# Block 0's first transform reads the raw rows: twelve products per column group and a wider table, in place of additions on VectorE and four products

## The chip, the cores and the metric

The kernel runs on one core of one Trainium2 chip. The metric is the device time of one execution in microseconds. The core has five engines that run side by side, each with a queue of its own that it works off in order: TensorE (PE; its weight loads are listed apart as PEld), VectorE (DVE), ScalarE (ACT), GpSimd (POOL) and SyncE (SP). In this kernel SyncE's queue issues almost all transfers between HBM and the on-chip memory; ScalarE's queue issues three at the start. Products land in PSUM, and VectorE or ScalarE must copy them out before their buffer is used again.

## The reference

The output mixes two branches over the same x (2048 rows of 512 numbers, bf16). One is a filter in the frequency domain, the other a layer norm followed by a two-layer network over the rows. A gate per row weighs them.

```python
x = A_x                                              # [1, 2048, 512]
g = sigmoid((x * gate_w).sum(-1, keepdims=True))
X = rfft2(x.astype(float32), axes=(-2, -1)) * (A_w_r + 1j * A_w_i)
a = irfft2(X, s=(2048, 512), axes=(-2, -1)).astype(bfloat16)
h = layernorm(x)
u = gelu(einsum("bsd,sf->bdf", h, w1) + b1)          # F = 1792
b = (einsum("bdf,fs->bds", u, w2) + b2).transpose(0, 2, 1)
out = g * a + (1 - g) * b
```

## The kernel before

The 2048 rows are split as `row = 512 q + 4 p + r`: p is the partition (0 to 127), and q and r run over 0 to 3. "Block r" is the 512 rows with the same r: four row tiles of 128 x 512, one for each q. Row tile j is 4 q + r. The kernel loads x block by block (`t["x"]`, L365 and L367), with the table of that block (`t["ta"]`, L368) and a part of w1 (`t["wa"]`, L378).

For each block four things are done:

- **Statistics and h.** VectorE takes mean and variance of each row tile (L462, L463). ScalarE takes the root (L472), VectorE the reciprocal and the shift (L476, L477). The normalised row tile h is written by VectorE for three row tiles (0, 8 and 4; L480) and by ScalarE for the other thirteen (L486).
- **Additions over q.** VectorE combines the four row tiles of a block by a radix-4 butterfly: two operations of 1024 elements (`q4a`, L494 and L495) and two of 512 (`q4b`, L500 and L501). The results stand in four parts of `t["xf", r]`, which lies in the not yet used end of the buffer `gl`.
- **First transform, over the rows (`fa`, L509 to L516).** For each column group dq (128 of the 512 columns) TensorE makes four products: the parts 2 and 3 with 256 table columns each, added in PSUM (L513, L514), and the parts 0 and 1 with 128 each (L515, L516). A PSUM buffer of the kind "fa" (there are two) holds the result of a group, and ScalarE copies it to `t["X"]` (L519).
- **Additions over column groups.** VectorE combines the copies (`d4a` and `d4b`, L526 to L533).

With all four blocks through, VectorE applies a radix-4 step to X for each of two halves lt (1, then 0; L552 to L565). The copy L603 then puts twelve small sums (L584 to L595) into the half lt = 0. Each of sixteen column transforms (`fb`, L621 to L624) puts four products into a buffer "fa" or "fb" (two each), which ScalarE copies to `t["B"]` (L628). Each half has eight of them; the half lt = 1 runs first.

The filter's weights come by many small transfers of SP (`ld_W`, two sets of eighteen). TensorE turns a part of them by a product with a flipped unit matrix (L706, into "fa" and "fb"), and ScalarE copies that out (L710). VectorE then prepares them (`wprep`: L726, L729, L730), multiplies B with them, and goes back over the columns; TensorE's inverse transforms are L838 to L845 over the rows and L912 to L916 over the columns.

The network's first layer is the products of L656 (`m1`), 224 of them with 512 columns, called **hidden products** here. Its sums lie in the PSUM buffers "acc" (four) and "fb" (two: the sums 4 and 5); ScalarE's Gelu empties them (L670). The first 72 hidden products run over twelve row tiles, two at a time, for the first six sums; the next 24 finish these six sums with block 3's row tiles. The second layer is L930 (`m2`), 238 products. The gate is made by VectorE (L679) and ScalarE's sums (L684).

Before the first transform TensorE runs warm-up products on zeros (`warm`, L353).

The order on every queue is fixed when the kernel is built. `add(engine, cost, emit, reads, writes, prio, ...)` records a task with an assumed cost; `Plan.order` plays the tasks through, and takes on each engine, of the tasks that are ready by the assumed costs, the one with the lowest `prio`. On the chip each engine then works through its own list in that order and waits where the data are not there. A change of one cost or `prio` can so move instructions anywhere behind it.

Of the kernel before, what the change touches and what calls it, by code (L numbers as in the profile page):

```python
# [28 lines left out]
    return np.ascontiguousarray(a.astype(ml_dtypes.bfloat16))  # L29


def ti_at(r):
    return (0, 1024, 512, 1920)[r], (512, 896)[r % 2]


def make_tables():

    p = np.arange(P)
    r4 = np.arange(4)
    alt = np.where(p % 2 == 0, 1.0, -1.0)  # L40

    def ang(rows, k, n):
        return 2 * np.pi * ((rows[..., None] * k) % n) / n

    ta = np.zeros((P, 4, 640))
    ti = np.zeros((P, 2946))
    for r in range(4):
        s = 4 * p + r
        for n, k0 in enumerate((0, 2)):
            th = ang(s, k0 + 4 * np.arange(64), S)  # L50
            ta[:, r, n * 128:n * 128 + 64] = np.cos(th)
            ta[:, r, n * 128 + 64:n * 128 + 128] = -np.sin(th)
        ta[:, r, 64] = alt
        th = ang(s, 1 + 4 * (p ^ 96), S)
        ta[:, r, 256:384] = np.cos(th)
        ta[:, r, 384:512] = -np.sin(th)
        ta[:, r, 512:640] = -np.cos(th)

        k = np.where(p < 64, 4 * p, 2 + 4 * (p - 64))
        o, w = ti_at(r)  # L60
        v = ti[:, o:o + w]
        if r % 2:
            sg = np.where(p < 64, 1.0, -1.0)[:, None]
            th = ang(k, s, S)
            v = v.reshape(P, 7, P)
            v[:, 0] = np.cos(th)
            v[:, 1] = sg * np.cos(th)
            v[:, 2] = -np.sin(th)
            v[:, 3] = -sg * np.sin(th)
            v[0, 2:4] = alt * (0.5 ** 0.5 if r == 1 else -(0.5 ** 0.5))  # L70
            th = ang(1 + 4 * (p ^ 96), s, S)
            v[:, 4] = -np.sin(th)
            v[:, 5] = np.cos(th)
            v[:, 6] = np.sin(th)
            ti[:, o:o + w] = v.reshape(P, w)
        else:
            s5 = np.append(s, 512)
            for lt, kk in enumerate((k, 1 + 4 * (p ^ 96))):
                th = ang(kk, s5, S)
                c, n = np.cos(th), -np.sin(th)  # L80
# [24 lines left out]
    tc[:, :, 2] = tc[:, :, 0]  # L105
    cf = np.zeros((P, 4, 2))
    m = np.arange(8).reshape(4, 2)
    for r in range(4):
        cf[m[0, 0], r, 0] = 1.0
        cf[8, r, 0] = (1.0, -1.0)[r % 2]  # L110
        cf[m[1, r % 2], r, 0] = (1.0, -1.0, -1.0, 1.0)[r]
        if r != 2:
            cf[m[2, 0], r, 1], cf[m[3, 0], r, 1] = 1.0, (1.0, -1.0)[r % 2]
        if r != 0:
            cf[m[2, 1], r, 1], cf[m[3, 1], r, 1] = (0.0, -1.0, 1.0, 1.0)[r], (0.0, -1.0, -1.0, 1.0)[r]
    tb = np.concatenate([tb[:, :, 0:2].reshape(P, 384), tc.reshape(P, 768), cf.reshape(P, 8)], 1)

    tg = np.zeros((P, 642))
    sc = 2.0 / (D * S)
    d = np.arange(129)  # L120
    for h in range(2):
        th = ang(2 * p + h, d, D)
        c, n = sc * np.cos(th), -sc * np.sin(th)
        if h == 0:
            c[0], n[0] = sc / 2, 0.0
            tg[:, 0:129], tg[:, 129:256] = c, n[:, 1:128]
        else:
            tg[:, 256:384], tg[:, 384], tg[:, 385:512] = c[:, 0:128], -n[:, 128], n[:, 1:128]
    tg[0, 512:641] = np.where(d % 2 == 0, 1.0, -1.0) * sc / 2
    return {"flip": bf(np.eye(P)[::-1]), "ta": bf(ta), "ti": bf(ti), "tb": bf(tb), "tg": bf(tg)}  # L130


# [103 lines left out]
def tt(n):  # L236
    return 0.07 + n / 1920.0
# [24 lines left out]
def kernel(  # L262
# [42 lines left out]
    def alloc_first():  # L305
        t["eps"] = sb([P, 1], F32, "eps")
        V.memset(t["eps"][:], 1e-5)
        t["x"] = sb([P, 4, 4, D], BF16, "x")
        t["h"] = sb([P, 4, 4, D], BF16, "h")
        t["X"] = sb([P, 2, 4, 2, 4, P], BF16, "X")  # L310
        t["B"] = sb([P, 2, 4, 4, L], BF16, "B")
        t["xp"] = sb([P, 8192], BF16, "xp")
        t["warm"] = t["xp"][:, 0:D]
        V.memset(t["warm"], 0.0)  # L314
        t["s9"] = sb([P, D], BF16, "s9")
        t["b1b"] = sb([P, P], BF16, "b1b")
        t["b2b"] = sb([P, D], BF16, "b2b")
        for k in ("s9", "b1b", "b2b"):
            V.memset(t[k][:], 0.0)
        t["st"] = sb([P, 4096], BF16, "st")  # L320
        t["gl"] = sb([P, NFT, D], BF16, "gl")
        t["W"] = sb([P, 2, 2, 4, 2, WL], BF16, "W")
        t["wn"] = sb([1, 2, WL], BF16, "wn")
        t["ta"] = sb([P, 4, 640], BF16, "rot")
        t["wt"] = sb([P, 2, 4, WL], BF16, "wt")
        t["wpm"] = sb([P, 2, 2, 4, 2], F32, "wpm")
        t["sp"] = sb([P, 4, 2, 4], F32, "sp")
        t["sd"] = sb([P, 2, 2, 2, 4], F32, "sd")
        t["fx"] = sb([P, 4, 2, 4], F32, "fx")
        t["c0"] = sb([P, 2, 4, 2, 2], F32, "c0")  # L330
        t["cm"] = sb([P, 4, 4, 2], F32, "cm")
        t["ce"] = sb([P, 2, 4, 2, 2], F32, "ce")
        for name, shape in (("stats", [P, NJ, nc.vector.BN_STATS_DIM]), ("mv", [P, NJ, nc.vector.BN_AGGR_DIM]),
                            ("rstd", [P, NJ]), ("nmr", [P, NJ]), ("glog", [P, NJ]), ("g", [P, NJ]), ("omg", [P, NJ]),
                            ("ombb2", [P, NJ]), ("b1f", [P, NFT]), ("b2f", [P, NJ])):
            t[name] = sb(shape, F32, name)
# [13 lines left out]
    def warm():  # L350
        pw = ps([P, D], F32, "fa", 2)
        for _ in range(NWARM):
            T.matmul(pw[:], lhsT=t["warm"][:, 0:P], rhs=t["warm"], start=True, stop=True)  # L353
    NWARM = 13
    add("PE", 0.42 * NWARM, warm, reads=["warm", "xs"], writes=["warmed"], prio=-5, alloc=["fa"], free=["fa"])

    def presq():
# [4 lines left out]
    for r in range(4):  # L362
        if r == 0:
            for q in range(4):
                ld([("x", 0, q)], lambda q=q: t["x"][:, q, 0, :], x4[:, q, 0, :], 131072, -9 + 0.1 * q, "SP" if q < 2 else "ACT")  # L365
        else:
            ld([("x", r, q) for q in range(4)], lambda r=r: t["x"][:, :, r, :], x4[:, :, r, :], 524288, 2 * r)  # L367
        ld([("ta", r)], lambda r=r: t["ta"][:, r, :], tabs["ta"][:, r, :], 163840, 2 * r + 0.2)  # L368

    NF = 6  # L370

# [7 lines left out]
        return emit  # L379

    for b in range(2):
        add(("SP", "ACT")[b], 0.5, ld_w1(0, slice(b, 4, 2), (None, A)[b]), writes=[("w1", 0, 4 * b), ("w1", 0, 4 * b + 8)], prio=(0.5, -4)[b],
            alloc=() if b else ["wa"], nbytes=393216, after=[a0])
    for r in range(1, 4):
        add("SP", 0.5, ld_w1(r), writes=[("w1", 0, 4 * q + r) for q in range(4)], prio=2 * r + 0.5, nbytes=786432)
# [61 lines left out]
    for r in range(4):  # L447
# [49 lines left out]
        def q4b(r=r):  # L497
# [1 line left out]
            s = t["st"][:, 0:1024].rearrange("p (m d) -> p m d", m=2)  # L499
            V.tensor_add(xf[:, 0], s[:, 0], s[:, 1])  # L500
            V.tensor_sub(xf[:, 1], s[:, 0], s[:, 1])  # L501
        if r == 0:
            add("DVE", 2 * tt(1024) + 2 * tt(512), lambda: (q4a(0), q4b(0)), reads=xk, writes=[("xf", 0), "st"], prio=-0.5, alloc=["xf"])
        else:
            add("DVE", 2 * tt(1024), q4a, reads=xk, writes=[("xf", r % 2), "st"], prio=1.2 * r + 0.6, alloc=["xf"])
            add("DVE", 2 * tt(512), q4b, reads=["st"], writes=[("xf", r % 2)], prio=1.2 * r + 0.6)

        for dq in range(4):
            def fa(r=r, dq=dq):  # L509
                pa = t["pa", r, dq] = ps([P, 2, 2, P], F32, "fa", 2)  # L510
                ta = t["ta"][:, r, :]
                w = lambda k: t["xf", r][:, k, dq * P:(dq + 1) * P]
                T.matmul(pa[:, 1], lhsT=w(2), rhs=ta[:, 256:512], start=True, stop=False)  # L513
                T.matmul(pa[:, 1], lhsT=w(3), rhs=ta[:, 384:640], start=False, stop=True)  # L514
                T.matmul(pa[:, 0, :, 0:64], lhsT=w(0), rhs=ta[:, 0:128], start=True, stop=True)  # L515
                T.matmul(pa[:, 0, :, 64:128], lhsT=w(1), rhs=ta[:, 128:256], start=True, stop=True)  # L516
            add("PE", mm(128, 128, 256, 256), fa, reads=[("xf", r % 2), ("ta", r)], writes=[("pa", r, dq)], prio=0, alloc=["fa"],
                free=["xf"] if dq == 3 else ())
            add("ACT", act(512), lambda r=r, dq=dq: A.copy(t["X"][:, :, r, :, dq, :], t["pa", r, dq][:]),  # L519
                reads=[("pa", r, dq)], writes=[("X", r, dq)], prio=0, free=["fa"])  # L520

# [491 lines left out]
```

## Time and profile before

| | us |
|---|---|
| median of 3 runs | 135.9 |
| lowest, highest | 135.12, 136.0 |
| the profiled execution, whole | 135.35 |
| span of the profiled execution (first to last instruction) | 133.3 |

The profile is of one execution. Times in it count from the first instruction. A row of the timeline has its start, its duration, the engine, the line of the kernel, the operation, output and inputs by name, how many instructions stand in the row, and in brackets how long the engine sat idle before it and what ended that. Operations of one kind overlap by their ends, so the pace of an engine is the distance between starts.

```profile
## 2 busy tenths in 40 slices
PE   6759999999999999999999999999999999999990
PEld 2244454545444666644445445557766756555590
DVE  2989999999999996399999999997797899999531
ACT  4047699999999999961111035326992966565200
POOL 0000000000000000000000000000000000000000
PEclk9999999999999999999999999999999999999999
DMA  4999999926499456999955900000000003304111
GB/s 133 277 363 392 391 391 380 272 61 135 79 308 360 90 126 174 317 362 416 424 223 193 417 25 2 0 2 5 0 0 0 5 0 157 130 27 162 50 69 38
```

Each digit is the busy share of a slice of 3.3 us in tenths. TensorE has its low slices at the start alone. VectorE is busy nearly throughout, ScalarE in the first half.

### The profile page before, as it was taken

The numbers are of one execution on the slowest core, as the hardware profiler recorded it, in microseconds if no ns is written. First come the engines' busy times: TensorE is split into PE (matmuls) and PEld (weight loads), VectorE is DVE, ScalarE is ACT, GpSimd is POOL, SyncE is SP. The second block draws the span as 40 slices with busy tenths as digits, with TensorE's granted clock in tenths as the row PEclk, the third lists the DMA queues.
The fourth block names the chain that finished last, engine by engine and source line by source line (L and its number), as shares of the span: only waits on it lengthen the run. The fifth ranks groups of instructions, "written<-read, shape, count | busy, mean of one in ns | idle before, by whom it ended". The sixth has DMA issues, their size and how long they took to land.

```text
span 133.3 us, 2162 instructions
## 1 busy us (share of the span) xinstructions
PE 125.3 (94%) x755; PEld 70.6 (53%) x769; DVE 115.0 (86%) x294; ACT 80.4 (60%) x155; POOL 0.2 (0%) x4
## 2 busy tenths in 40 slices
PE   6759999999999999999999999999999999999990
PEld 2244454545444666644445445557766756555590
DVE  2989999999999996399999999997797899999531
ACT  4047699999999999961111035326992966565200
POOL 0000000000000000000000000000000000000000
PEclk9999999999999999999999999999999999999999
DMA  4999999926499456999955900000000003304111
GB/s 133 277 363 392 391 391 380 272 61 135 79 308 360 90 126 174 317 362 416 424 223 193 417 25 2 0 2 5 0 0 0 5 0 157 130 27 162 50 69 38
DMA packets 17206, 23.18 MB, mean 174 GB/s; under 512 B 1174, under 2 KB 14636, under 8 KB 17196
## 3 DMA queue, kind: packets, MB, share of 16 engines
q1 hardware_dynamic: 16636, 22.39, 49.4%
q10 hardware_dynamic: 560, 0.66, 1.4%
q8 instruction: 6, 0.10, 0.3%
q14 instruction: 4, 0.03, 0.1%
HBM read 20.93 MB, written 2.10 MB: 173 GB/s over the span
## 4 chain that ended last, share of the span: by engine, by line
PE 54%; DMA 33%; SPq 8%; issue 2%; DVE 0%
PE acc L930 29%; PE acc L656 13%; DMA wa<-in_B_w_dram 11%; SPq L303 8%; DMA wt<-in_A_w_i_dram 6%; DMA wb<-in_B_w_dram 6%; DMA s<-X 5%; DMA W<-in_A_w_r_dram 4%; DMA W<-in_A_w_i_dram 2%; PE fa L838 1%; PE fb L838 1%; PE fa L930 1%; PE fa L624 1%; PE fb L624 1%; PE fa L912 1%
## 5 line engine op out<-in xcount | busy, mean ns | idle before, releaser
L930 PE MATMUL acc<-gl,wb 128*128 128x512 bf16 (+1 forms) x123 | 31.0, 373 | 0.3
L656 PE MATMUL acc<-h,wb 128*128 128x512 bf16 x124 | 28.8, 379 | 0.2
L930 PE MATMUL acc<-gl,wa 128*128 128x512 bf16 (+1 forms) x94 | 23.4, 372 | 0.1
L930 PEld LDWEIGHTS <-wb 128*128 128x128 bf16 x136 | 14.9, 114 | 10.4 <-DMA wb<-in_B_w_dram 0.3
L656 PEld LDWEIGHTS <-wb 128*128 128x128 bf16 x128 | 12.5, 98 | 13.5
L656 PE MATMUL acc<-h,wa 128*128 128x512 bf16 x62 | 16.8, 379 | 1.4 <-DMA wa<-in_B_w_dram 1.1
L950 ACT ACTIVATE x<-acc,ombb,omg 128x512 bf16<-128x512 f32 x14 | 10.7, 777 | 10.3 <-PE acc L930 10.3
L930 PEld LDWEIGHTS <-wa 128*128 128x128 bf16 x102 | 11.5, 114 | 8.4
L656 PEld LDWEIGHTS <-wa 128*128 128x128 bf16 x96 | 9.1, 98 | 10.5 <-DMA wa<-in_B_w_dram 1.3
L670 ACT ACTIVATE gl<-acc,b1f 128x512 bf16<-128x512 f32 x12 | 8.5, 706 | 9.6 <-PE acc L656 9.6
L462 DVE BATCH_NORM_STATS2 stats<-x 128x6 f32<-128x512 bf16 x16 | 10.8, 673 | 2.2 <-DMA x<-in_A_x_dram 2.2
L519 ACT CAST X<-fa 128x512 bf16<-128x512 f32 x16 | 8.8, 583 | 3.3 <-PE fa L516 3.2
L486 ACT ACTIVATE h<-x,nmr,rstd 128x512 bf16<-128x512 bf16 x13 | 9.8, 806 | 1.2 <-DVE nmr L477 1.2
L684 ACT ACTIVATE x<-x 128x512 bf16<-128x512 bf16 x16 | 10.2, 668 | 0.0
L656 PE MATMUL fb<-h,wa 128*128 128x512 bf16 x31 | 9.0, 379 | 0.0
L921 ACT ACTIVATE eo<-fa,g 128x512 bf16<-128x512 f32 x8 | 5.5, 685 | 5.4 <-DVE x L956 3.7
L353 PE MATMUL fa<-xp 128*128 128x512 bf16 x13 | 4.5, 520 | 1.2 <-DVE xp L314 1.2
L513 PE MATMUL fa<-rot,gl 128*128 128x256 bf16 x16 | 4.4, 272 | 1.3 <-DMA rot<-dft_ta 1.2
L809 ACT CAST s<-fa 8x512 bf16<-8x512 f32 x1 | 0.6, 574 | 8.2 <-PE fa L807 8.2
L921 ACT ACTIVATE eo<-fb,g 128x512 bf16<-128x512 f32 x8 | 5.5, 683 | 0.0
L956 DVE TENSOR_TENSOR x<-x,eo 128x512 bf16<-128x512 bf16 x14 | 5.3, 417 | 0.0
L628 ACT CAST B<-fb 128x512 bf16<-128x512 f32 x8 | 5.2, 647 | 0.0
(167 smaller groups left out, 230.8 us busy)
## 6 DMA issues: line engine op xcount, KB each, us to landing
wb<-in_B_w_dram SPq DMA_DIRECT2D x8, 512.0 KB
wb<-in_B_w_dram SPq DMA_DIRECT2D x4, 1024.0 KB
wa<-in_B_w_dram SPq DMA_DIRECT2D x3, 1024.0 KB
wa<-in_B_w_dram SPq DMA_DIRECT2D x3, 768.0 KB
x<-in_A_x_dram SPq DMA_DIRECT2D x3, 512.0 KB
out_dram<-x SPq DMA_DIRECT2D x3, 512.0 KB
rot<-dft_ti SPq DMA_DIRECT2D x1, 736.5 KB
rot<-dft_ta SPq DMA_DIRECT2D x4, 160.0 KB
```

The lines of the kernel that those rows point to most:

```text
L303: (eng or nc.sync).dma_start(out=out_ap, in_=in_ap)
L462: V.bn_stats(out=t["stats"][:, j, :], in_=t["x"][:, j // 4, j % 4, :])
L486: add("ACT", act(512, 2), lambda j=j: A.activation(t["h"][:, j // 4, j % 4, :], t["x"][:, j // 4, j % 4, :], ActF.Identity, bias=t["nmr"][ ...
L519: add("ACT", act(512), lambda r=r, dq=dq: A.copy(t["X"][:, :, r, :, dq, :], t["pa", r, dq][:]), reads=[("pa", r, dq)], writes=[("X", r, dq ...
L628: A.copy(t["B"][:, lt, e, 2 * c:2 * c + 2, :].rearrange("p s (i b) -> p s i b", b=4), t["pb", lt, e, c][:].rearrange("p s b i -> p s i b"))
L656: T.matmul(t["u", ft][:], lhsT=w[:, j // 4, j % 4, c * P:(c + 1) * P], rhs=t["h"][:, j // 4, j % 4, :], start=(j == jorder[0]), stop=(j == ...
L670: gelus.append(add("ACT", act(512, 1), lambda ft=ft: A.activation(t["gl"][:, ft, :], t["u", ft][:], ActF.Gelu_apprx_tanh, bias=t["b1f"][:, ...
L684: A.activation(t["x"][:, q, r, :], t["x"][:, q, r, :], ActF.Copy, accum_out=t["glog"][:, 4 * q + r:4 * q + r + 1])
L921: A.activation(t["eo", j][:], t["i3", j][:], ActF.Copy, scale=t["g"][:, j:j + 1])
L930: T.matmul(t["y", j, n][:, cs], lhsT=w[:, o, 512 * q + r:512 * q + 512:4], rhs=t["gl"][:, ft, cs], start=(ft == 0), stop=(ft == NFT - 1))
L950: A.activation(tbuf(j).rearrange("p h d -> p (h d)"), t["y", j, 0][:], ActF.Identity, bias=t["ombb2"][:, j:j + 1], scale=t["omg"][:, j:j + 1])
L956: V.tensor_add(o, o, t["eo", j][:])
```

## The change

Only block 0's first transform is computed in another way. Its additions over q (L494 to L501 for r = 0) are gone. TensorE takes the raw row tiles of x as weights, and the signs and turns that the additions and four products made now stand in the table. For each column group there are twelve products: four with 128 columns for part 0 (all with the same table columns, one for each q), four with 128 for part 1 (the table columns with alternating sign), and four with 256 for parts 2 and 3 together (each q takes table columns that begin 128 further on). Block 0's table has 1024 columns in place of 640 (262,144 B in place of 163,840), the others stay. The warm-up has 9 products in place of 13. The assumed cost of block 0's groups, and two `prio`, change with it.

```diff
-    ta = np.zeros((P, 4, 640))
+    ta = np.zeros((P, 4, 1024))
...
         ta[:, r, 512:640] = -np.cos(th)
+        ta[:, r, 640:768] = np.sin(th)
+        ta[:, r, 768:896] = np.cos(th)
+        ta[:, r, 896:1024] = -ta[:, r, 128:256]
...
-    NWARM = 13
+    NWARM = 9
...
-        ld([("ta", r)], lambda r=r: t["ta"][:, r, :], tabs["ta"][:, r, :], 163840, 2 * r + 0.2)
+        ld([("ta", r)], lambda r=r: t["ta"][:, slice(*ta_at(r))], tabs["ta"][:, slice(*ta_at(r))], 163840 if r else 262144, 2 * r + 0.2 if r else -8)
...
-        add(("SP", "ACT")[b], 0.5, ld_w1(0, slice(b, 4, 2), (None, A)[b]), writes=[("w1", 0, 4 * b), ("w1", 0, 4 * b + 8)], prio=(0.5, -4)[b],
+        add(("SP", "ACT")[b], 0.5, ld_w1(0, slice(b, 4, 2), (None, A)[b]), writes=[("w1", 0, 4 * b), ("w1", 0, 4 * b + 8)], prio=(-7, -4)[b],
...
-        if r == 0:
-            add("DVE", 2 * tt(1024) + 2 * tt(512), lambda: (q4a(0), q4b(0)), reads=xk, writes=[("xf", 0), "st"], prio=-0.5, alloc=["xf"])
-        else:
+        if r:
             add("DVE", 2 * tt(1024), q4a, reads=xk, writes=[("xf", r % 2), "st"], prio=1.2 * r + 0.6, alloc=["xf"])
             add("DVE", 2 * tt(512), q4b, reads=["st"], writes=[("xf", r % 2)], prio=1.2 * r + 0.6)
...
+                if r == 0:
+                    w = [t["x"][:, q, 0, dq * P:(dq + 1) * P] for q in range(4)]
+                    f = [dict(start=q == 0, stop=q == 3) for q in range(4)]
+                    for q in range(4):
+                        T.matmul(pa[:, 0, :, 0:64], lhsT=w[q], rhs=ta[:, 0:128], **f[q])
+                    for q in range(4):
+                        T.matmul(pa[:, 0, :, 64:128], lhsT=w[q], rhs=ta[:, 128:256] if q % 2 == 0 else ta[:, 896:1024], **f[q])
+                    for q in range(4):
+                        T.matmul(pa[:, 1], lhsT=w[q], rhs=ta[:, 256 + 128 * q:512 + 128 * q], **f[q])
+                    return
...
-            add("PE", mm(128, 128, 256, 256), fa, reads=[("xf", r % 2), ("ta", r)], writes=[("pa", r, dq)], prio=0, alloc=["fa"],
-                free=["xf"] if dq == 3 else ())
+            add("PE", mm(128, 128, 256, 256) * (1 if r else 2.6), fa, reads=[("xf", r % 2) if r else ("x", 0, q) for q in range(4)] + [("ta", r)],
+                writes=[("pa", r, dq)], prio=0, alloc=["fa"], free=["xf"] if dq == 3 and r else ())
```

The planner moves other instructions with it. What differs in the order of the two kernels (lines of the kernel before):

- **TensorE.** Before, two groups of block 0 stood first and the other two between the first hidden products; now all 48 products of block 0 stand in a row ahead of the first hidden product. Block 1's transform begins after 25 hidden products (before 30), block 2's after 43 (47), block 3's after 75 (81). The two flips of L706 for the first set of weights stand together after hidden product 96 (before after 95 and 97). The first set of column transforms begins after 131 (137), the second after 150 (152). The inverse transforms begin after 91 products of the second layer (92).
- **VectorE.** The four additions are gone; the statistics of a few row tiles stand in another order around block 1's additions. The copy L603 stands behind `wprep` (L726 to L730) in place of ahead of it.
- **ScalarE.** The table load for Gelu stands behind the first two of block 3's four copies L519 (before ahead of all four); some of the gate's sums L684 stand elsewhere.
- **SyncE.** The order of the transfers is the same; the first table is larger.

More of the change, by code (lines that the diff above doesn't have):

```diff
@@ L29, in bf, with ta_at @@
     return np.ascontiguousarray(a.astype(ml_dtypes.bfloat16))
+def ta_at(r):
+    return (1024 + 640 * (r - 1), 1024 + 640 * r) if r else (0, 1024)
 def ti_at(r):
@@ L129, in make_tables @@
     tg[0, 512:641] = np.where(d % 2 == 0, 1.0, -1.0) * sc / 2
+    ta = np.concatenate([ta[:, 0]] + [ta[:, r, 0:640] for r in range(1, 4)], 1)
     return {"flip": bf(np.eye(P)[::-1]), "ta": bf(ta), "ti": bf(ti), "tb": bf(tb), "tg": bf(tg)}
@@ L323, in alloc_first @@
         t["wn"] = sb([1, 2, WL], BF16, "wn")
-        t["ta"] = sb([P, 4, 640], BF16, "rot")
+        t["ta"] = sb([P, 2944], BF16, "rot")
         t["wt"] = sb([P, 2, 4, WL], BF16, "wt")
@@ L510, in fa @@
                 pa = t["pa", r, dq] = ps([P, 2, 2, P], F32, "fa", 2)
-                ta = t["ta"][:, r, :]
+                lo, hi = ta_at(r)
+                ta = t["ta"][:, lo:hi]
+                if r == 0:
[8 more added lines that the diff above has]
+                    return
                 w = lambda k: t["xf", r][:, k, dq * P:(dq + 1) * P]
```

## The prediction

> **What bounds the kernel now.** I read the page first (busy us of each engine), then TensorE's waits (us in total, times, longest), then the timeline where the change moves work (start, us, what, and in brackets the idle time before it).
>
> ```profile
> PE 125.3 (94%) x755; PEld 70.6 (53%) x769; DVE 115.0 (86%) x294; ACT 80.4 (60%) x155; POOL 0.2 (0%) x4
> ```
> ```profile
> PE fa L513 <- DMA rot<-dft_ta: 1.2, 1, 1.2
> PE acc L656 <- DMA wa<-in_B_w_dram: 1.1, 1, 1.1
> ```
>
> A busy share of 94% could hide stalls, since ends of products are modelled, so I measured by starts: a 512-column product follows the last after 0.2155 us, a 256-column one after 0.11, a 128-column one after 0.055. From 12.39 to the end all starts beyond these paces add up to only 2.4 us. TensorE is the bound: work added there is paid, unless it fills a gap. The gaps are at the start:
>
> ```profile
> 4.18 1.03 PEld L353 LDWEIGHTS <-xp 128*128 128x128 bf16 x5 [0.28 <-issue]
> ...
> 6.91 0.27 PE L513 MATMUL fa<-rot,gl 128*128 128x256 bf16 x1 [1.21 <-DMA rot<-dft_ta]
> ...
> 8.85 0.39 PE L656 MATMUL acc<-h,wa 128*128 128x512 bf16 x1 [1.12 <-DMA wa<-in_B_w_dram]
> ...
> 12.39 1.02 PE L656 MATMUL acc<-h,wa 128*128 128x512 bf16 x4
> ```
>
> The transform waits for its table until 6.91; the weight load on the additions' result stood ready at 6.45. Two groups are over at 7.57 (the last product starts at 7.51), and TensorE waits 1.28 us for weights. At 12.11 (two products from 11.68) it waits 0.28 us for the h that L480 writes from 11.93.
>
> ```profile
> 5.12 0.68 DVE L494 TENSOR_TENSOR st<-x 128x1024 bf16<-128x1024 bf16 x1
> ...
> 10.06 0.69 DVE L462 BATCH_NORM_STATS2 stats<-x 128x6 f32<-128x512 bf16 x1 [0.46 <-DMA x<-in_A_x_dram]
> ```
>
> VectorE already waits 0.46 us at 10.06 for block 1's rows.
>
> **Table.** SP issues in the same order as before. The table is 98,304 B larger, and all on SP's queue behind it (w1, block 1's rows, later loads) comes later: at 402 GB/s (9 to 10 us) by 0.25 us, at 272 (5 to 6 us) by 0.36. I take 0.3 for the first product (7.2) and 0.25 behind it; bounds 0, if the queue has room, to 0.7 (half rate beside ScalarE's queue).
>
> **Products.** Old group: 2 x 0.11 + 2 x 0.055 = 0.33, four 1.32. New group: 8 x 0.055 + 4 x 0.11 = 0.88, four 3.53. More work: 2.21 us. The pace holds in long runs: ten 128-column products at 90.32 to 90.83 stand 0.057 apart. The transform runs 7.2 to 10.73; weights land by 9.1, so the 1.28 is filled. Twelve hidden products (L656) later, at 13.3, the h that made the 0.28 is there (block 1's rows at 10.3, one set of statistics 0.81, reciprocals and h 0.8: 11.9). Net: 0.3 + 2.21 - 1.28 - 0.28 = +0.95.
>
> **VectorE.** The four additions leave: 1.87 us (5.12 to 6.99, where the next row starts). Nothing comes of it: without them VectorE is through with block 0 at 7.7 (9.60 less 1.87) and waits for block 1's rows until 10.3. Its queue reorders, but by the block 1 additions it has done the same set, 0.25 later than before. The cover is the transfer; where that goes, see the third rival.
>
> **Block 1 and 2 transforms.** TensorE reaches block 1's after 25 hidden products, at 10.73 + 5.39 = 16.12. The last addition ended at 16.34, now 16.59: 0.2 us wait in the first group. The third group needs the copy of the first out of PSUM, and ScalarE does two h first (15.71, now 15.96), so the copy comes at 17.39 and the group at 18.0 against 17.41: 0.6. Before, the waits there were 0.17 and 0.15. Change +0.48. Block 2's, likewise, 0.45 for 0.29: +0.16. Shift so far 1.59.
>
> **ScalarE around block 3.** In the order before, the Gelu table load stood before the four copies of block 3 and ran while ScalarE had nothing else; now two copies stand ahead of it.
>
> ```profile
> 28.72 1.28 ACT L670 ACT_TABLE_LOAD   x1
> 30.02 1.38 ACT L670 ACTIVATE gl<-acc,b1f 128x512 bf16<-128x512 f32 x2
> 31.35 1.75 ACT L519 CAST X<-fa 128x512 bf16<-128x512 f32 x3
> ...
> 35.23 0.70 ACT L670 ACTIVATE gl<-fb,b1f 128x512 bf16<-128x512 f32 x1
> ```
>
> Hidden product 73 was at 28.78, now 30.37; after three more block 3's first group starts at 31.02 (before 30.72, its copy 0.63 later at 31.35). So copies at 31.65 and 32.15, load 32.65 to 33.95, then by ScalarE's starts a Gelu 0.57, two copies 0.94, two Gelus 1.14, a gate sum 0.61, a Gelu 0.57: the first Gelu of an fb buffer starts at 37.78 and ends at 38.48. The flip of L706 into fb needs that buffer. TensorE is there at 37.2 (31.02, four groups and twenty-one hidden products, and the flip into fa) and waits 1.3; before, with the flip at 35.99, 0.1. Behind it in TensorE's queue stand all further hidden products. Flip and product 97 were over at 36.20, now 38.93: shift 2.73. If the copies did not hold up the load, this term is 0.
>
> **The copy of L603.** Before it stood ahead of W's preparation; now behind it, and the second set of transforms over columns (L621) needs it.
>
> ```profile
> 50.99 0.24 DVE L603 CAST X<-fx 128x32 bf16<-128x32 f32 x1
> 52.15 0.42 DVE L726 TENSOR_SCALAR W<-W 1x1028 bf16<-1x1028 bf16 x1 [0.92 <-ACT x L684]
> ...
> 53.01 0.16 DVE L758 TENSOR_TENSOR cm<-c,wpm 128x8 f32<-128x8 f32 x1
> ```
>
> It now starts where L758 did, at 53.01, or 53.26 with the queue's 0.25, and ends by 53.5. TensorE, with two hidden products fewer ahead (150, not 152), arrives at 51.52 (its first product of that set now) + 2.73 - 0.43 = 53.82. So it costs nothing, by 0.3 us. But it is a floor: were the earlier waits nothing, TensorE would stand until 53.25 to 53.5, and with the two products still owed the shift is 2.2 to 2.4. ScalarE's last copies of that set move by about as much (56.06 to 58.7), so VectorE's chain to the inverse transforms shifts with TensorE.
>
> **Warm-up.** Four products fewer, before the table is there: nothing, unless the clock is late. The weight loads of L353 start 0.43 us apart up to the one at 4.18, and the last five take 1.03 us together; nine products at 0.43 end at 5.0, so it comes in time here. The gap to 7.2 is 2.2 us; gaps of 1.2 and 1.3 us before slowed nothing, and no row shows one of 2.2. The Trainium skill ("TensorE: Matmul & The Clock Gate", Part 1) says that full clock comes after a window of some 3.4 us of sustained work, that the window runs freely, and that a whole idle window takes it away. By that rule the gap is harmless, but nine products (3.9 us) hardly cover a window, which speaks against this edit; what it would cost is rival 1.
>
> **Sum.** 0.95 + 0.48 + 0.16 + 1.14 = 2.73, less 0.1 for small gaps that close: +2.6 us on a span of 133.3, 135.9. The profiled execution took 135.35 (2.05 us around its span), within the runs shown (135.12 to 136.0), whose median is 135.9. Forecast: 135.9 + 2.6 = 138.5.
>
> **Rivals.**
> 1. Late clock. If full clock has not come by 5.0, the transform starts at half pace and gets it 3.1 us after its first product (as now: 1.21 to 4.3): at 10.3 it has done 1.55 us of its 3.53, and ends at 12.3 instead of 10.7. Waits of 0.2 are absorbed: +1.4, 139.9. For: 0.43 us starts until 4.18, and now only nine products. Against: here it came at the eighth. It decides if it comes later than 5.0. Chance 0.13.
> 2. Only work counts: ScalarE's load slips in earlier, W's preparation too, and later gaps swallow the rest: +0.95, 136.85. For: 2.4 us of gaps from 12.39 on. Against: two separate waits, either of them worth over 2 us in all, would both have to fail. Chance 0.12.
> 3. Faster: VectorE's 1.87 us comes through. Its place is the wait at 10.06. If block 1's rows land by 8.2, VectorE runs all of it ahead, h and additions are early, and TensorE's 2.4 us of gaps close: 0.95 - 2.4 = -1.45, 134.45. Against: the rows stand behind table and weights in one queue, and W's preparation, which the transfers set, stays. Chance 0.08.
>
> The forecast's own case has 0.67; its range is 137.8 (the floor of L603, less small gaps) to 139.3 (table 0.7, longer copies).
>
> **Numbers.** Time 138.5. The range 136.8 to 140.1 takes in the own range and rivals 1 and 2, and leaves out some 0.1 below and 0.06 above. One per cent, about what a measurement here can tell from no change, is 1.36 us: slower by more are the forecast and the late clock, 0.80; within it rival 2, 0.12; faster 0.08.
>
> **What would show it.** First L527 or L523 product on `x` near 7.2 and the 48 over by 10.8, pace 0.055 (0.11 would be the late clock); no wait for wa; VectorE idle 2 us before block 1's statistics; the table load near 32.6 with TensorE waiting over 1 us at the fb flip; the copy into X (now L620) after 53. Wrong would be: products on raw rows slower than 0.055, block 1's rows landing near 8, or a table load that runs before block 3's copies.

## The result: 140.28 us, slower by 3.3 %

| | before | after |
|---|---|---|
| median, us (6 runs each) | 135.88 | 140.28 |
| lowest, highest | 135.12, 136.53 | 139.49, 141.1 |
| profiled execution, whole | 135.35 | 140.75 |
| its span | 133.3 | 138.5 |

The ratio is 1.0329, with a 95 % interval from 1.0277 to 1.0381. The sign was right; the size was not. The range ended at 140.1. A median in this text is of all runs of a kernel; a ratio leaves out those that took over 1.5 % more than the fastest run of the same kernel.

In the changed kernel lines have moved down: by 8 near L353, by 17 from L519 on (L656 is L673, L670 is L687, L706 is L723). Two views answer to the first ones of before. The page's busy times (us, share of the span, instructions), after:

```profile
PE 129.1 (93%) x783; PEld 74.5 (54%) x797; DVE 113.5 (82%) x290; ACT 80.3 (58%) x155; POOL 0.2 (0%) x4
```

TensorE's waits (us in total, times, longest), after:

```profile
PE fa L523 <- DMA rot<-dft_ta: 2.6, 1, 2.6
PE fb L723 <- ACT gl L687: 1.2, 1, 1.2
```

VectorE lost 1.5 us of work and TensorE gained 3.8. The wait for weights is gone, the wait for the table went from 1.2 to 2.6 us, and a wait at the flip into fb is new. Together these waits add 1.5 us (1.4 and 1.2 more, 1.1 less), and the span grew by 5.2. The rest is in TensorE's own time: 2.21 us more products were reckoned with, and the pace is the other part, of which the shorter warm-up and gaps that closed take some back. The timeline of after (start, us, what, idle time before it):

```profile
7.86 0.58 PE L523 MATMUL fa<-rot,x 128*128 128x128 bf16 x4 [2.62 <-DMA rot<-dft_ta]
8.24 0.63 PE L525 MATMUL fa<-rot,x 128*128 128x128 bf16 x4
8.67 1.06 PE L527 MATMUL fa<-rot,x 128*128 128x256 bf16 x4
...
12.93 0.61 PE L523 MATMUL fa<-rot,x 128*128 128x128 bf16 x4
13.36 0.40 PE L525 MATMUL fa<-rot,x 128*128 128x128 bf16 x4
13.60 0.60 PE L527 MATMUL fa<-rot,x 128*128 128x256 bf16 x4
14.04 0.38 PE L673 MATMUL acc<-h,wa 128*128 128x512 bf16 x1
```

Read the distance between starts. Four 128-column products take 0.43 us (8.24 to 8.67) until 13.36, then 0.24 (to 13.60), and four 256-column ones then take 0.44 (to 14.04): TensorE ran at half pace for all but the last eight of the 48 products. They took 6.18 us (7.86 to 14.04) where 3.53 were forecast. The trace's record of the clock says the same: full speed was granted at 4.31 before the change, and at 13.38 after it.

The later steps, in the same timeline:

```profile
10.76 0.70 DVE L470 BATCH_NORM_STATS2 stats<-x 128x6 f32<-128x512 bf16 x1 [3.03 <-DMA x<-in_A_x_dram]
...
34.07 1.07 ACT L536 CAST X<-fa 128x512 bf16<-128x512 f32 x2 [2.64 <-PE fa L533]
35.16 1.28 ACT L687 ACT_TABLE_LOAD   x1
36.45 0.69 ACT L687 ACTIVATE gl<-acc,b1f 128x512 bf16<-128x512 f32 x1
...
39.46 0.38 PE L723 MATMUL fa<-wt,flip 128*128 128x256 bf16 x2
...
40.32 0.72 ACT L687 ACTIVATE gl<-fb,b1f 128x512 bf16<-128x512 f32 x1
...
41.09 0.38 PE L723 MATMUL fb<-wt,flip 128*128 128x256 bf16 x2 [1.25 <-ACT gl L687]
...
54.96 0.42 DVE L743 TENSOR_SCALAR W<-W 1x1028 bf16<-1x1028 bf16 x1 [1.02 <-DMA W<-in_A_w_i_dram]
...
55.83 0.24 DVE L620 CAST X<-fx 128x32 bf16<-128x32 f32 x1
...
56.37 0.22 PE L638 MATMUL fa<-tb,X 128*128 128x128 bf16 x1
```

VectorE now waits 3.03 us for block 1's rows, more than the 1.87 us it was spared. Two copies stand ahead of the Gelu table load, so the first Gelu of an fb buffer starts at 40.32 and the flip waits for it: the two products of the flip into fa (39.46) take 0.22, and the flip into fb starts 1.41 us after their end by that pace. The copy into X starts at 55.83, behind W's preparation, and TensorE reaches the products that need it at 56.37 without a wait.

### The profile page after: what moved, and what is told of

It is laid out like the page before. It is cut to its first block, busy times and chain, and to the rows that moved or that the text cites. A ratio compares the mean times of both kernels' runs of the same rounds, so it can differ in the third digit from the quotient of the medians.

```text
span 138.5 us, 2213 instructions
## 1 busy us (share of the span) xinstructions
PE 129.1 (93%) x783; PEld 74.5 (54%) x797; DVE 113.5 (82%) x290; ACT 80.3 (58%) x155; POOL 0.2 (0%) x4
## 4 chain that ended last, share of the span: by engine, by line
PE 72%; DMA 9%; ACT 8%; DVE 5%; issue 2%; SPq 2%; ACTq 0%
PE acc L947 28%; PE acc L673 23%; DMA rot<-dft_ta 4%; DMA s<-X 4%; ACT h L494 3%; PE fa L527 2%; DVE stats L470 2%; ACT gl L687 2%; SPq L311 2%; ACT X L536 2%; PE fb L673 2%; PE fa L855 1%; PE fa L523 1%; PE fb L855 1%; PE fb L641 1%
## 5 line engine op out<-in xcount | busy, mean ns | idle before, releaser
L673 PE MATMUL acc<-h,wb 128*128 128x512 bf16 x124 | 28.3, 379 | 0.1
L673 PEld LDWEIGHTS <-wb 128*128 128x128 bf16 x128 | 12.5, 98 | 13.5
L673 PE MATMUL acc<-h,wa 128*128 128x512 bf16 x63 | 17.0, 379 | 0.1
L687 ACT ACTIVATE gl<-acc,b1f 128x512 bf16<-128x512 f32 x12 | 8.4, 710 | 10.0 <-PE acc L673 10.0
L673 PEld LDWEIGHTS <-wa 128*128 128x128 bf16 x96 | 9.1, 98 | 9.1
L494 ACT ACTIVATE h<-x,nmr,rstd 128x512 bf16<-128x512 bf16 x13 | 9.9, 806 | 1.2 <-DVE nmr L485 1.2
L673 PE MATMUL fb<-h,wa 128*128 128x512 bf16 x30 | 8.6, 379 | 0.1
L645 ACT CAST B<-fa 128x512 bf16<-128x512 f32 x8 | 5.2, 652 | 0.0
L361 PE MATMUL fa<-xp 128*128 128x512 bf16 x9 | 4.0, 631 | 1.2 <-DVE xp L322 1.2
```

The lines of the kernel that those rows point to most:

```text
L494: add("ACT", act(512, 2), lambda j=j: A.activation(t["h"][:, j // 4, j % 4, :], t["x"][:, j // 4, j % 4, :], ActF.Identity, bias=t["nmr"][ ...
L645: A.copy(t["B"][:, lt, e, 2 * c:2 * c + 2, :].rearrange("p s (i b) -> p s i b", b=4), t["pb", lt, e, c][:].rearrange("p s b i -> p s i b"))
L673: T.matmul(t["u", ft][:], lhsT=w[:, j // 4, j % 4, c * P:(c + 1) * P], rhs=t["h"][:, j // 4, j % 4, :], start=(j == jorder[0]), stop=(j == ...
L687: gelus.append(add("ACT", act(512, 1), lambda ft=ft: A.activation(t["gl"][:, ft, :], t["u", ft][:], ActF.Gelu_apprx_tanh, bias=t["b1f"][:, ...
```

## The experiments

The theories of where the time went: the late clock; the later landing of the wider table; the Gelu load behind block 3's copies; and, against them, products on raw rows that are slow by themselves, or VectorE's new order. On the chip of the first four experiments the kernel before took 135.33 (19 runs).

**Warm-up, 13 and 22 products.** Both kernels are the changed one, with the planned order kept.

```diff
-    NWARM = 9
-    add("PE", 0.42 * NWARM, warm, reads=["warm", "xs"], ...
+    NWARM = 13
+    add("PE", 0.42 * 9, warm, reads=["warm", "xs"], ...
```

> The changed kernel with its 13 warm-up products of before, every queue in the changed kernel's order. Theory (the clock): nine products end at 5.0 and leave TensorE idle to 7.9, and what the change costs beyond my sum of +2.6 us is the transform at half pace. With 13 the products last to 5.5 to 6.8; full clock should come by 6 and the 48 products run at 0.055 and 0.11: 3.5 us, 138.0 to 138.6 us. If the idle stretch up to the table takes the clock away whatever the count, some executions still lose 1.5 to 2 us: 139 to 140.3. Rival (the products on raw rows are slow by themselves, because x is read as weights while VectorE reads it): no change, 140.3 us, pace 0.107 and 0.213.

Measured: 140.11 (138.1 to 140.75, 4 runs), ratio 1.0255 (1.0139 to 1.0371). Thirteen are not enough: three of the four runs show a mean granted clock of 0.985 to 0.988 and took 139.9 to 140.8. The fourth, at 1.000, took 138.1, which is what the theory gave for a clock that stays. The page has no row for a taken clock, but a table by windows does (stretch in us; its length, TensorE's busy time and instructions; granted clock; DMA share; GB/s):

```profile
1.64:5.05 3.41, 3.41 (x10) 1.00 0.86 250
5.05:8.47 3.42, 1.44 (x13) 1.00 0.98 319
8.47:11.88 3.41, 3.41 (x28) 0.50 1.07 390
```

Here the warm-up filled a stretch of 3.41 us and the clock was granted at 5.05. In the next stretch TensorE was busy for 1.44 us only, waiting for the table until 8.06, and the clock was taken away for 3.41 us, in which most of the transform ran (8.06 to 13.23). (A stretch that has no record yet prints 1.00, so a first number of 1.00 says nothing.)

With 22 in place of 13:

> The changed kernel with 22 warm-up products, order unchanged, so that TensorE has no idle stretch before the table (8 at 0.43 and 14 at 0.2155 end near 7.7). Theory (the clock): the transform runs at full pace in every execution, 138.0 to 138.6 us, mean granted clock at least 0.998 in all runs; the same or faster than with 13. Rival (slow by themselves): 140.3 us, pace 0.107 and 0.213. If warm-up products delay the transform, its first product comes after the table and the time is up to 0.3 us longer.

Measured: 139.0 (138.75 to 139.34), ratio 1.026 (1.0191 to 1.0328). The timeline of this kernel:

```profile
8.54 0.39 PE L523 MATMUL fa<-rot,x 128*128 128x128 bf16 x4
8.77 0.39 PE L525 MATMUL fa<-rot,x 128*128 128x128 bf16 x4
8.99 0.60 PE L527 MATMUL fa<-rot,x 128*128 128x256 bf16 x4
9.43 0.39 PE L523 MATMUL fa<-rot,x 128*128 128x128 bf16 x4
```

A group of twelve takes 0.89 us (8.54 to 9.43), and the whole transform 3.54 (to 12.08). So raw rows are not slow by themselves. The warm-up itself ran on for 0.57 us after the table had landed (7.97), which this kernel pays.

**The two suspects alone, on the kernel before.** Nine warm-up products instead of 13; and a table of 1024 columns of which 640 are used, so that only its transfer grows.

```diff
-    NWARM = 13
-    add("PE", 0.42 * NWARM, warm, ...
+    NWARM = 9
+    add("PE", 0.42 * 13, warm, ...
```

> The kernel before with 9 warm-up products in place of 13, order unchanged: one part of the change alone. Theory (the clock): idle from 5.0 to 6.9 and again to 8.85, so the clock comes late or is taken away here too; the start is half hidden by waits for weights, and 12 to 20 hidden products run at half pace: 136.5 to 138.0 us. Rival (the count does not matter): 135.9 us.

```diff
-    ta = np.zeros((P, 4, 640))
+    ta = np.zeros((P, 4, 1024))
...
+    ta = np.concatenate([ta[:, 0]] + [ta[:, r, 0:640] for r in range(1, 4)], 1)
...
-                ta = t["ta"][:, r, :]
+                ta = t["ta"][:, ta_at(r)[0]:ta_at(r)[0] + 640]
```

> The kernel before with block 0's table 1024 columns wide, of which it uses 640: one part of the change alone. My sum's term: the table lands 0.3 us later, weights and block 1's rows 0.25 later; TensorE waits for weights anyhow, so +0.25 us: 136.1. Rival (the table costs what the changed kernel's profile shows, first product 0.95 us later, for which my term was too small): the table lands near 7.8, weights near 9.4, time +0.5 to +0.9: 136.4 to 136.8.

Measured: 136.26 for nine warm-up products, ratio 1.0058 (1.0029 to 1.0087); 136.14 for the table, ratio 1.005 (1.0021 to 1.0079). Each costs the kernel before 0.8 to 0.9 us by the medians (10 runs each). With nine products the clock came at 13.23, but there most of the half pace hides behind the waits for table and weights that this kernel has anyway. The wide table's last part landed at 8.02 instead of 6.87, and the wait for it took away, at 8.55, the clock that had come at 5.14. So the two suspects meet: a later table makes the idle stretch longer, and the idle stretch takes the clock.

**The Gelu load.** The kernel before took 135.16 (13 runs) beside this run and the next three. To the kernel with 22 warm-up products, one small activation is added behind block 3's last normalized rows.

```diff
+    add("ACT", 0.0, lambda: A.activation(t["ombb2"][:, 0:1], t["eps"][:], ActF.Gelu_apprx_tanh, bias=t["eps"][:, 0:1], scale=1.0),
+        reads=[("h", 4 * q + 3) for q in range(4)], prio=-2)
```

> The kernel with 22 warm-up products (139.0), and a Gelu over one column right behind block 3's last normalized rows on ScalarE, so that the Gelu table is loaded ahead of block 3's copies and not between them. Theory (that load stands on TensorE's path where the work turns to block 0's second matrix): the gap of TensorE there falls from 1.41 us to 0.3 us or less, VectorE's preparation of W, which waited for ScalarE's copy of W, comes earlier by about as much, the second set of column transforms still starts without a gap, and the time falls by 1.1 to 1.3 us, to 137.7 to 137.9, 2.4 us above the kernel before. Rival (TensorE then waits for the copy of the column sums instead): the gap there goes, one of 0.7 to 1 us appears ahead of the second set of column transforms at 53 us, and the time falls by 0.3 to 0.5 us only, to about 138.6.

Measured: 137.98 (137.39 to 141.44, 4 runs), ratio 1.0162 (1.0079 to 1.0246), just above what the theory gave (137.7 to 137.9). Its timeline:

```profile
29.49 1.28 ACT L693 ACT_TABLE_LOAD   x1
30.79 0.29 ACT L693 ACTIVATE ombb<-eps 128x1 f32<-128x1 f32 x1
32.11 1.07 ACT L536 CAST X<-fa 128x512 bf16<-128x512 f32 x2 [1.03 <-PE fa L533]
...
37.51 0.38 PE L726 MATMUL fa<-wt,flip 128*128 128x256 bf16 x2
37.73 0.38 PE L726 MATMUL fb<-wt,flip 128*128 128x256 bf16 x2
37.94 3.40 PE L673 MATMUL acc<-h,wb 128*128 128x512 bf16 x15
```

The load now runs while ScalarE has nothing to do, and the flip into fb follows the one into fa after 0.22 us: the gap of 1.41 us is gone. Nothing took its place before the second set of column transforms.

> The same with VectorE's copy of the column sums put ahead of its preparation of W. If the copy's margin of 0.3 us is used up by the earlier Gelu load, this kernel is faster than the one without it by 0.7 to 1 us (137.6 to 137.9 against 138.6). If the copy never stood on the path, the two differ by less than 0.3 us.

```diff
-        writes=[("Z", 0, 0), ("Z", 0, 1)], prio=3.1)
+        writes=[("Z", 0, 0), ("Z", 0, 1)], prio=0.9)
```

Measured: 136.67 (136.04 to 137.21, 10 runs), ratio 1.0094 (1.0057 to 1.0131). By the medians it is 1.3 us below the last one, which is neither of the two cases expected, but the profiled spans are the same (135.2). This run's transform started 0.4 us earlier (7.57 against 7.97), it reached the second set at 51.85 instead of 53.01, and later waited 0.9 us for the transfer of s, at another place in the order. It moves too much to tell the copy's share; the last pair of experiments does that.

**VectorE's additions put back.** They are executed again in the kernel with 22 warm-up products, and nothing reads them.

```diff
+        if r == 0:
+            add("DVE", 0.0, lambda: (q4a(0), q4b(0)), reads=xk, writes=[("xf", 0), "st"], prio=-0.5)
```

> The kernel with 22 warm-up products, and VectorE makes block 0's additions again, though nothing reads them (1.9 us of work put back, everything else in its order). Theory (VectorE's relief is worth nothing, because it waits 3.4 us for block 1's rows right behind): the wait of VectorE for block 1's rows falls from 3.43 us to about 1.6 us, all later work stands where it stood within 0.1 us, and the time stays at 139.0, 3.6 us above the kernel before. Rival (the relief comes through somewhere): up to 1.9 us more, 140 to 140.9.

Measured: 138.63, ratio 1.0226 (1.0151 to 1.03), against 1.026 without them. Its timeline:

```profile
4.99 0.68 DVE L502 TENSOR_TENSOR st<-x 128x1024 bf16<-128x1024 bf16 x1
...
6.52 0.42 DVE L509 TENSOR_TENSOR gl<-st 128x512 bf16<-128x512 bf16 x1
...
9.39 0.66 DVE L470 BATCH_NORM_STATS2 stats<-x 128x6 f32<-128x512 bf16 x1
```

The 1.87 us of work are there, and VectorE then goes on to block 1's statistics without a wait (I had expected 1.6 us of it to be left; in this run the rows were there by 9.39). The time did not rise: the upper end of the ratio, 1.03 of 135.16, is 139.2, below the rival's 140. In this kernel the relief of VectorE is worth nothing that four runs can measure. This profile does not show that the wait for rows is the cover, since block 1's rows had landed at 9.22 in it, against 10.90 in the kernel with 22 warm-up products.

**The table first.** The changed kernel with its nine warm-up products; the table is issued ahead of the first two row transfers on the same queue, and nothing else moves.

```diff
+        def emit():
+            for d, s in (((t["ta"][:, slice(*ta_at(0))], tabs["ta"][:, slice(*ta_at(0))]),) if keys[0] == ("x", 0, 0) else ()) + (((dst(), src),) if keys[0] != ("ta", 0) else ()): dma(d, s, A if eng == "ACT" else None)
```

> The changed kernel with its 9 warm-up products, and the first table's transfer issued ahead of the two row transfers on the same queue instead of behind them (nothing else moves). Theory (the wider table's last part and the idle stretch ahead of it cost 1 us and the clock): table and rows have all landed by 6 to 6.9 us, the first product starts 1 to 1.9 us earlier than 7.86; the idle stretch is then 1 to 1.9 us, and if the clock is granted in time (the groups of 12 products 0.88 us apart) the time falls by 2 to 4 us, to 136.3 to 138.3. If the clock still comes late (groups 1.7 us apart), it falls by 1 to 2 us, to 138.3 to 139.3. Rival (whichever transfer comes last on the queues lands at 7 to 8 us, whatever it carries): the first product stays at 7.5 to 8 us, now waiting for the rows, and the time stays at 140.

Measured: 138.32 (137.13 to 144.17, 4 runs), ratio 1.0159 (1.0044 to 1.0274). Its timeline:

```profile
5.03 0.31 PE L523 MATMUL fa<-rot,x 128*128 128x128 bf16 x1
6.03 0.50 PE L523 MATMUL fa<-rot,x 128*128 128x128 bf16 x3 [0.69 <-DMA x<-in_A_x_dram]
6.33 0.63 PE L525 MATMUL fa<-rot,x 128*128 128x128 bf16 x4
```

The table has landed whole at 4.14 and the last row transfer at 5.98: together they are there 1.8 us before the table alone was in the changed kernel (7.82). The first product, at 5.03, follows the warm-up without a wait; the second waits for that last row transfer. The pace is still the half one, until 10.05. That is the theory's second case, 138.3 to 139.3.

**Table and Gelu early together, 13 warm-up products.** Beside this and the next one the kernel before took 135.4 (11 runs).

> The changed kernel with three parts put together: the table's transfer ahead of the rows (as in the run of that alone, where the products started at 6.03), the early Gelu (gap of 1.4 us gone), and 13 warm-up products in place of 9, which last until the data come. If the late clock, the table's last part and the Gelu load are the three terms that made the change dear, their shares add: products from 6.0 to 6.5 us at full pace (groups of twelve 0.88 us apart). The transform of block 1 then has a floor: it started 7.69 us after block 1's rows had landed in the two kernels where it waited (10.82 and 18.51; 10.52 and 18.21), so with rows at 9.93 it starts no earlier than 17.6, about 1 us before the 18.64 of the kernel with 22 warm-up products. Time 0.9 us below the early Gelu alone (2.0 % above before): 136.0 to 137.0, ratio 1.006 to 1.013. Rival (another wait takes over later, at the transfer of s near 80 us or at VectorE's preparation of W): no better than 137 to 137.5.

Measured: 137.74 (137.36 to 139.91, 6 runs), ratio 1.0163 (1.0124 to 1.0201): the gain did not come through, and the rival had it right. The transform ran from 6.61 to 10.10 at full pace, as expected, and the third group of block 1's transform started at 17.58, 7.69 us after the rows (it waits for ScalarE's copy of the first group, and ScalarE normalizes those rows first). But then:

```profile
52.00 0.42 DVE L746 TENSOR_SCALAR W<-W 1x1028 bf16<-1x1028 bf16 x1 [1.05 <-DMA W<-in_A_w_i_dram]
...
52.85 0.24 DVE L620 CAST X<-fx 128x32 bf16<-128x32 f32 x1
...
53.15 0.23 PE L638 MATMUL fa<-tb,X 128*128 128x128 bf16 x1 [0.91 <-DVE cm L778]
```

W's preparation waits for its transfer until 52.00, the copy into X is queued behind it on VectorE, and TensorE, which is now early, stands until 53.15. (The view names L778, which stands directly behind the copy; the products read X, which the copy writes.) This is the floor that the prediction spoke of.

**Block 1's rows ahead of the weights.** The two transfers change places in SyncE's queue.

```diff
-            dma(t["wa"][:, qs, r, :], w1v[:, qs, r, 0:FA], eng)
+            dma(*((t["wa"][:, qs, r, :], w1v[:, qs, r, 0:FA]) if r or eng else (t["x"][:, :, 1, :], x4[:, :, 1, :])), eng)
```

> The same with block 1's rows issued ahead of the first half of block 0's weights on the same queue (the two transfers change places). If block 1's rows are the floor of block 1's transform, they land at 8.5 to 9.3 us instead of 9.9, the wait ahead of that transform (about 1 us) shrinks by as much, and the time falls by another 0.5 to 1 us, to 135.3 to 136.3, level with the kernel before (ratio 1.000 to 1.007). Rival (the weights, now later, make the first hidden product wait, or a later wait eats it): the two differ by less than 0.2 us.

Measured: 138.89 (136.78 to 140.8, 6 runs), ratio 1.0151 (1.0094 to 1.0207), no better. VectorE no longer waited for those rows and block 1's wait was gone; TensorE met the floor earlier and stood there for 2.01 us. The same table by windows shows what that did:

```profile
47.53:50.94 3.41, 3.41 (x22) 1.00 0.71 165
50.94:54.35 3.41, 1.40 (x16) 1.00 0.69 235
54.35:57.76 3.41, 3.41 (x20) 0.50 0.83 293
```

In the middle of the kernel, one wait of 2 us was followed by 3.41 us at half pace. It does not happen in every execution: three of the six runs, the profiled one (139.38) among them, show a mean clock of 0.985 to 0.988 and took 139.4 to 140.8; the other three, at 0.996 to 1.000, took 136.8 to 138.4.

**The copy ahead of W's preparation**, nothing else moved, in each of the last two kernels; the kernel before took 135.08 (17 runs) beside them.

```diff
-        W, pm = t["W"], t["wpm"]
+        W, pm = t["W"], t["wpm"]; V.tensor_copy(t["X"][:, 0, :, :, :, 0], t["fx"][:])
...
-    add("DVE", 0.15, lambda: V.tensor_copy(t["X"][:, 0, :, :, :, 0], t["fx"][:]), reads=["fx"],
+    add("DVE", 0.15, lambda: None, reads=["fx"],
```

> The kernel with both early (table, Gelu) and 13 warm-up products, and VectorE's copy of the column sums put directly ahead of its preparation of W, nothing else moved. Before the second set of column transforms TensorE waited there for 1.07 us, because the copy was queued behind the preparation of W, which waited for a transfer until 52.0 us. Theory (the copy behind W is a floor at about 53.1 us for whatever gains time earlier): the gap goes, the second set starts at about 52.1, and the time falls by 0.9 to 1.1 us, to 136.6 to 136.9 beside a kernel before of 135.4 (ratio 1.008 to 1.012). Rival (a later floor, the transfer of s near 80 us, takes it): a gap of up to 1 us near 79 us, and the time stays within 0.3 us of 137.7.

Measured: 136.11 (135.56 to 136.35, 6 runs), ratio 1.0086 (1.0054 to 1.0118). Against the ratio without it, 1.0163, that is 1.0 us, as the theory gave. The second set starts at 51.87 without a gap.

> The same copy ahead, in the kernel whose block 1 rows are issued ahead of the weights. There the gap was 2.17 us, and TensorE ran at half pace for 3.41 us right behind it. Theory: with the gap gone the clock stays, the last product comes 2.2 to 3.9 us before 133.51, at 129.6 to 131.3, and the time is 135.0 to 136.4, the kernel before 135.4. That is 0.5 to 1 us below the kernel without the earlier rows. Rival (the transfer of s near 80 us is the floor): the two end alike within 0.3 us.

Measured: 135.38 (135.05 to 135.69, 12 runs), ratio 1.0029 (1.0007 to 1.0052). Its timeline:

```profile
49.72 0.24 DVE L745 CAST X<-fx 128x32 bf16<-128x32 f32 x1
...
50.95 0.22 PE L638 MATMUL fa<-tb,X 128*128 128x128 bf16 x1
...
51.04 0.42 DVE L746 TENSOR_SCALAR W<-W 1x1028 bf16<-1x1028 bf16 x1 [1.08 <-DMA W<-in_A_w_i_dram]
```

W's preparation still waits for its transfer, but the copy is done before it and TensorE goes on at 50.95. So with the table, the clock, the Gelu load, block 1's rows and the copy all seen to, twelve products on raw rows come out 0.3 % above the kernel before. What is left there is the next wait: the third groups of block 1's and 2's transforms stand 0.52 and 0.40 us for ScalarE's copies of the first, which ScalarE does after it has normalized rows. The first hidden product waits 0.27 us as well, for weights that now land behind the rows, at 9.37. No version here beats the kernel before.

## Why the prediction was wrong

**The step that failed** is the warm-up: "Four products fewer, before the table is there: nothing, unless the clock is late". The clock was late. I read off that nine products at 0.43 us end at 5.0, after the clock of before had come at 4.31, and took that for in time. What decides in these traces is how full a stretch of 3.41 us is, about 80 % to get the clock, and afterwards how full the next one is (the table at the end). Nine products fill 4.0 us (1.22 to 5.24), and whether one stretch holds enough of them depends on where its borders fall: in the profiled run they split into 1.94 us before 3.15 and 2.09 us behind it, and the clock came at 13.38. The idle time from 5.24 to 7.86 can take a clock that did come. Of the six runs, the four fastest show a mean clock of 0.987 or 0.988, which is what one stretch at half leaves (half of 3.41 us of 130 is 1.3 %), as in the kernel with 13; no trace of them is kept, so this is read from the mean alone. The first rival was this case, with 0.13 of the chance and 139.9 us. It was still too kind: it let the full clock come 3.1 us after the transform's first product, and it came after 5.5.

By the page that the prediction's paragraph on the warm-up names, the Trainium skill ("TensorE: Matmul & The Clock Gate", Part 1), a whole idle window takes the clock away, so I called the gap of 2.2 us harmless. The traces do not agree: windows in which TensorE was busy for 1.44 and 1.40 of 3.4 us took it. The page's other statement, a freely running window of some 3.4 us of sustained work before full clock, agrees with the records in the length of the window and in its borders, which fall elsewhere in each run; four fifths of a window were enough work.

**The table** was mis-sized: "I take 0.3 for the first product (7.2)". It came at 7.86, 0.95 later than before and outside the bounds of 0 and 0.7. I scaled the added bytes by the core's mean rate. The first product needs the last of the sixteen parts in which the transfer landed, and the delay of the slowest part was not that of the mean: in before the parts landed from 4.26 to 6.87 with half of them by 4.6, in after the last one at 7.82. Why the last parts come so late is not shown.

**The block 1 and 2 transforms** cost nothing instead of 0.48 and 0.16. TensorE left block 0's transform 3.3 us later than I had reckoned (14.04 for 10.73) and found the copies done: the two gaps are 0.075 and 0.264 us. Where TensorE came early, in the kernel with table and Gelu early, they are 0.52 and 0.40, close to the 0.6 and 0.45 of the prediction.

**Right** were: the products' pace at full clock (3.54 against 3.53 us), the weights' and h's waits gone, VectorE's relief worth nothing (the additions put back cost nothing that could be measured), the Gelu load on the path (a gap of 1.41 us, forecast 1.3; its early load took the gap away), and the copy as a floor (TensorE did not wait for it in after, and stood 1.07 and 2.17 us in the two kernels that came to it early enough). That its margin came out at the forecast 0.3 us is luck: the copy started at 55.83 and not at 53.26, because W's preparation waited for a transfer that SyncE issued 2.5 us later than before (the last one of the set at 52.99 against 50.48), and TensorE was late by as much (56.37 for 53.82).

The sum by measured terms: the forecast span 135.9, plus 2.65 for the pace (6.18 less 3.53), plus 0.65 for the table (7.86 less 7.2), plus 0.1 at the flip, less 0.73 and 0.19 for the waits at blocks 1 and 2 (0.075 and 0.264 found, 0.8 and 0.45 forecast), is 138.4; the profiled span is 138.5. Without the late clock, the kernel with 22 warm-up products took 139.0, of which 0.57 are warm-up that overran: 138.4, where the forecast was 138.5. That they meet so closely is luck: the kernel before took 135.33 beside it and not the 135.9 that the forecast started from, so the change cost 3.1 us there, 0.5 more than the 2.6 forecast, and the table's 0.65 is of that size.

Not tried: the additions put back where VectorE waits for no rows (the last kernel above). There the relief may be worth something. Nor was the kernel before given the table first or the earlier rows; the early Gelu load and the copy ahead it has already. So the 0.3 % compares the twelve products with two transfers moved against four products without that, and what the twelve products alone are worth stays open. VectorE's and ScalarE's new orders were not put back as a whole.

## What to carry to other kernels

Warm-up products are part of the clock's budget, not padding: before taking any out, or before making the wait that follows them longer, look at what fills the stretch of 3.4 us before and after, since the price is paid in another place, at half pace. When a transfer grows, ask for its last part and not for its mean rate. And where two steps of one queue change places, find out which of them waits for a transfer: what stands behind it inherits that wait as soon as the rest of the kernel gets faster.

## What the runs showed of the hardware

How full a stretch of 3.41 us must be (busy time by the modelled ends of the products, borders by the clock's records):

| kernel, stretch | TensorE busy | clock |
|---|---|---|
| before, 0.90 to 4.31 | 3.10 (91 %) | half, then granted |
| copy ahead, without the earlier rows, 0.53 to 3.94 | 2.73 (80 %) | half, then granted |
| table first, 3.23 to 6.64 | 2.72 (80 %) | half, not granted |
| nine warm-up products in before, 6.40 to 9.82 | 2.57 (75 %) | half, not granted |
| after, 6.56 to 9.97 | 2.11 (62 %) | half, not granted |
| table and Gelu early, 4.03 to 7.44 | 2.42 (71 %) | full, kept |
| before, 4.31 to 7.72 | 2.20 (65 %) | full, kept |
| table and Gelu early, 130.32 to 133.73 | 1.64 (48 %) | full, kept |
| wide table in before, 5.14 to 8.56 | 1.48 (43 %) | full, taken away |
| 13 warm-up products, 5.05 to 8.47 | 1.44 (42 %) | full, taken away |
| rows ahead, 50.94 to 54.35 | 1.40 (41 %) | full, taken away |

So a stretch 48 % full was enough to keep the clock and one 75 % full not enough to get it. In these runs the bound for getting it lies near 80 %, and that for losing it between 43 and 48 %, as far as the modelled ends can tell. The borders follow a fixed step: the stretches at full clock on record last 3.41, 47.79, 78.51, 122.88, 126.29, 129.71 and 133.12 us, which are 1, 14, 23, 36, 37, 38 and 39 times 3.413.

The kernel before is near the edge itself. Of its 19 runs beside the first four experiments three show a mean clock of 0.987 and took 136.0 to 136.4, where the median is 135.33.

The last part of the table landed at 7.5 to 8.0 us in six of seven profiled kernels that load 1024 columns behind the rows, and at 5.73 in one, while the same bytes issued first were there at 4.0 to 4.2 in all five. With 640 columns behind the rows it was 6.87 in both profiled kernels. The place in the queue moved it by more than 3 us (that one kernel aside), and 0.1 MB more by about 1.
